# Attention backward over a KV cache: the last stores on GpSimd's queue, and a second-pass head beside each of the first pass's last two rows

## The chip, the cores and the metric
The kernel runs on one core of a Trainium2 chip. The metric is the device time of one execution in microseconds; 922.77 us is the median of three runs (921.22 to 922.89). Engines are named as the profile names them: PE (TensorE matmul), PEld (its weight load), DVE (VectorE), ACT (ScalarE), POOL (GpSimd) and SP (SyncE, which here only issues DMAs).

## What is computed
The reference is a decode step and its gradient. The forward part, cut to what matters:

```python
q = (layernorm(x) @ wq)                      # per head: 1 x 128
scores = einsum("bhqd,bhkd->bhqk", q, k) * Dh**-0.5
p = softmax(scores)
o = einsum("bhqk,bhkd->bhqd", p, v)
h = x + o @ wo
h2 = h + relu(layernorm(h) @ w1) @ w2        # the output
```

With B = 2, H = 32 heads of 128, and 4096 cached positions there are 64 pairs of batch and head, and each pair's K and V are 1 MB in bfloat16. `jax.vjp` asks for the gradients of all inputs. The two large ones have the shapes of the caches: gV is, for each pair, the outer product of p and the gradient of o; gK is the outer product of the scores' gradient and q. So 128 tiles of 1 MB are written, beside the gradients of wq, wo, w1 and w2 and that of x.

## The kernel before
The work on the caches has two passes, each going over the 64 pairs.

**First pass.** Row i loads K of pair i, and works on three pairs at once: the scores of pair i (PE transposes of K at L418, copies at L423, products at L429), the softmax and the scaled K of pair i-1 (`pk`, L480), and the sums over V of pair i-2 (`m_ps` L473, `u_ps` L502). So it has 66 rows, 0 to 65; the rows 64 and 65 only finish the last pairs. When V has been used, its tile goes back, or is kept for the second pass (the last 6 heads of batch 0 and the last 5 of batch 1).

**Second pass.** Head j (`p2_iter`, L848) reads V again as `W`, transposes it in pairs (L439), and multiplies it with the gradient of o (L452) for the scores' gradient `gsp` (L856). Then VectorE makes the two outer products in halves of about 1.2 us (`outer_half`, L834): in the call for head j, first gK of head j-1, then gV of head j. Each finished tile is stored by one DMA of 128 rows of 8 KB. `store_tile` (L839) chooses the queue: POOL while the list `queue` of loads still to be issued has entries, SP once it is empty. For the gK of heads 60, 61 and 62 it issues two DMAs, of rows 0 to 119 and of rows 120 to 127.

**What sets the order.** The order of all instructions is written by hand. `plan` (L1081 to L1089) pairs first-pass rows with second-pass heads: from row 41 on every second row has a head beside it (rows 41, 43, ..., 65 with heads 0 to 12), and when the first pass is over, from row 66 on, each row is one head. A closing row 64 of the second pass makes the last gK. From the same plan comes `queue` (L1092 to L1110), the order of the loads, which `pump` (L1111) issues on SP as soon as a load tile is free.

Loads and stores share a set of 1 MB tiles, which `share` hands out by use: `ld` for loads, `g` for gK and gV, `f` and `q` for the final gradients. The store tiles number three in the rows around 64, five from row 66 on (L1154), and seven from head 43 on (L1165). A tile is taken again in the order in which tiles were given back, and the instruction that writes it waits until its store has landed.

Beside the heads, background work is spread over the rows: the middle part of batch 1 (`middle_gen`), the outer products for the weights' gradients (`fin_gen`, L958, stored from ACT at L955), and the gradient of x (`gx_gen`, L983, with the products `ttr` of L660 on VectorE and two small stores at L655).

Of the kernel before, what the change touches and what calls it, by code (L numbers as in the profile page):

```python
# [15 lines left out]
def kernel(  # L16
# [20 lines left out]
    nc = tc.nc  # L37
# [35 lines left out]
    def pst(shape, dtype, role, name):  # L73

        k = banks[role].pop(0)
        banks[role].append(k)
        return ps.tile(shape, dtype, tag=f"bank{k}", bufs=1, name=name)
# [11 lines left out]
    def take(tag, shape, name):  # L89
        assert free[tag] > 0, (tag, name)  # L90
        free[tag] -= 1
        k = homes[tag].pop(0)
        t = pools[k].tile(shape, BF16, tag=f"big{k}", bufs=1, name=name)
        home_of[id(t)] = (tag, k, t)
        return t
# [9 lines left out]
    def give(t, to=None):  # L105
        tag, k, _ = home_of.pop(id(t))
        to = to or goes_to(tag)
        owned[tag] -= 1
        owned[to] += 1
        free[to] += 1  # L110
        homes[to].append(k)
        given_at[k] = step[0]
# [280 lines left out]
    NP1 = len(pairs)  # L393
# [37 lines left out]
    def pair_transpose(nat, g, dve=False, busy=0):  # L431


        t_ps = pst([128, GT // 2, 128], FP32, "tps", "t_ps")
        warm(t_ps[:].rearrange("p j k -> p (j k)"), nat, g, busy)
        natf = nat[:].bitcast(FP32)
        for j in range(GT // 2):
            cc = (g * GT) // 2 + j
            nc.tensor.transpose(t_ps[:, j, :], natf[:, 2 * cc:2 * cc + 2, :].rearrange("p c k -> p (c k)"), ident_f[:])  # L439
        t_sb = mats.tile([128, GT // 2, 128], FP32, tag="XT", bufs=5, name="t_sb")  # L440
        if dve:
            nc.vector.tensor_copy(out=t_sb[:], in_=t_ps[:])
        else:
            nc.scalar.copy(out=t_sb[:], in_=t_ps[:])  # L444
        return t_sb

    def pair_matvec(dst, t_sb, g, vecs):
        v = t_sb[:].bitcast(BF16).rearrange("p j (k two) -> p j k two", two=2)
        for j in range(GT // 2):
            sc = g * GT + 2 * j  # L450
            for par in range(2):
                nc.tensor.matmul(dst[:, sc:sc + 2], lhsT=v[:, j, :, par], rhs=vecs[:, par, :],  # L452
                                 start=(par == 0), stop=(par == 1))

    def natural(cache, b, h):
        return cache[b, h].rearrange("(p sc) d -> p sc d", sc=NSC)
# [375 lines left out]
    def outer_half(dst, row, colp, k):  # L832
        sl = slice(k * HALF, (k + 1) * HALF)
        nc.vector.tensor_tensor(  # L834
            out=pairs_view(dst[:, sl, :]),
            in0=row.rearrange("p (a two) -> p a two", two=2)[:, None, :, :].to_broadcast([128, HALF, 64, 2]),
            in1=colp[:, sl, None, :].to_broadcast([128, HALF, 64, 2]), op=ALU.mult)

    def store_tile(dst, t, uneven=False):  # L839

        eng = nc.gpsimd if queue else nc.sync
        if uneven:
            eng.dma_start(out=dst[0:120], in_=t[0:120])
            eng.dma_start(out=dst[120:128], in_=t[120:128])
        else:
            eng.dma_start(out=dst, in_=t[:])  # L846

    def p2_iter(j, busy):  # L848

        c = S2[j] if j < NP1 else None  # L850
        p = S2[j - 1] if j >= 1 else None
        if p is not None:
            bp, hp = turns[j - 1]
            pair_matvec(p["dp"], p.pop("T3"), 3, gom[:, hp, bp, :, :])
            gsp = small.tile([128, NSC, 2], BF16, tag="gsp", name="gsp")
            nc.vector.scalar_tensor_tensor(  # L856
                out=gsp[:], in0=p["dp"][:, :, None].to_broadcast([128, NSC, 2]), scalar=negdot[:, hp, bp:bp + 1],
                in1=P_bf[:, bp * H + hp, :, None].to_broadcast([128, NSC, 2]), op0=ALU.add, op1=ALU.mult)
        if c is not None:
            b, h = turns[j]  # L860
            go = gom[:, h, b, :, :]

            bank = pst([128, 512], FP32, "sps", "dp_ps")
            for k, col in enumerate((goc, qsc)):
                nc.tensor.matmul(bank[:, 128 + k * 128:256 + k * 128],  # L865
                                 lhsT=col[:, h, b:b + 1].to_broadcast([128, 128]), rhs=ident_bf[:],
                                 start=True, stop=True)
            c["dp"] = bank[:, 0:NSC]
            rb = mats.tile([128, 256], BF16, tag="rb", bufs=4, name="rb")
            nc.scalar.activation(out=rb[:], in_=bank[:, 128:384], func=ACT.Copy, scale=rt[:, b, h:h + 1])  # L870
            pp = small.tile([128, NSC, 2], BF16, tag="pp", name="pp")
            nc.gpsimd.tensor_copy(out=pp[:], in_=P_bf[:, b * H + h, :, None].to_broadcast([128, NSC, 2]))
            c.update(rb=rb, pp=pp)
            c["T0"] = pair_transpose(c["W"], 0, busy=busy)
        if p is not None:
            gK = take("g", [128, NSC, 128], "gK")
            outer_half(gK, p["rb"][:, 128:256], gsp, 0)
        yield
        if p is not None:
            outer_half(gK, p["rb"][:, 128:256], gsp, 1)  # L880
            store_tile(natural(out_2, bp, hp), gK, NP1 - 4 <= j - 1 < NP1 - 1)
            give(gK)
            del S2[j - 1]
        yield
        if c is None:
            return
        c["T1"] = pair_transpose(c["W"], 1, busy=busy)
        pair_matvec(c["dp"], c.pop("T0"), 0, go)
        yield
        c["T2"] = pair_transpose(c["W"], 2, busy=busy)  # L890
        pair_matvec(c["dp"], c.pop("T1"), 1, go)
        yield
        c["T3"] = pair_transpose(c["W"], 3, busy=busy)
        give(c["W"], "g" if j < H and j != 1 and owned["g"] < 3 else None)
        pair_matvec(c["dp"], c.pop("T2"), 2, go)
        gV = take("g", [128, NSC, 128], "gV")
        outer_half(gV, c["rb"][:, 0:128], c["pp"], 0)
        yield
        outer_half(gV, c["rb"][:, 0:128], c["pp"], 1)
        store_tile(natural(out_3, b, h), gV)  # L900
        give(gV)
        yield

# [173 lines left out]
    P2_AT = H + 2 + M0_ITERS  # L1077
# [4 lines left out]
    i = j = 0  # L1082
    while i <= NP1 + 1 or j <= NP1:
        ii = i if i <= NP1 + 1 else None
        jj = j if i > NP1 + 1 or (i >= P2_AT and (i - P2_AT) % 2 == 0) else None
        plan.append((ii, jj))
        i += 1
        if jj is not None:
            j += 1  # L1089


    queue = []  # L1092
# [51 lines left out]
    for n, (i, j) in enumerate(plan):  # L1144
# [21 lines left out]
        if j is not None:  # L1166
            while g2 is not None:
                p2_step()
            if j < NP1:
                bg_until(("go", *turns[j]))  # L1170
            g2 = p2_iter(j, 0)
# [93 lines left out]
```

## Time and profile before

| what | value |
|---|---|
| median of three runs | 922.77 us |
| the profiled execution | 922.89 us, span 921.1 us |
| busy share: PE, DVE, ACT, POOL | 82%, 75%, 58%, 18% |
| granted TensorE clock, mean | 0.771 |
| moved by DMA | 363.00 MB, mean 394 GB/s |
| read from HBM, written to it | 212.16 MB, 149.13 MB |
| gV and gK stores issued from POOL | 57 and 57, median 14.7 and 14.0 us to landing |
| gV stores issued from SP | 7, median 10.1 us to landing |
| VectorE waits for a stored tile | 18.3 us before gK, 17.9 us before gV |

The first column of a timeline row is the start in microseconds from the start of the span, the second the duration. In a table by stage each row is a stretch of the span; behind the busy times of the five engines come the granted TensorE clock, the mean busy share of the 16 DMA engines, and the rate in GB/s. A share may come out a little over 1, since successive packets overlap by a few nanoseconds. Queue q0 (software_dynamic) is POOL's, q1 (hardware_dynamic) SP's, and q10 ACT's. "Landing" is the time from a DMA's issue until its semaphore is complete, which takes all its engines.

### The profile page before, as it was taken

To read this page: it belongs to the slowest core of one execution; us is meant where nothing else is said; L and a number is where in the kernel's file an instruction comes from. 1 tells how busy PE (TensorE), PEld (TensorE's weight loads), DVE (VectorE), ACT (ScalarE), POOL (GpSimd) and SP (SyncE) were. 2 spreads that over 40 slices of the span, in tenths; PEclk is the share of its full clock that TensorE was granted. 3 is DMA by queue.
4 is the path that set the end of the run, shared out by engine and by line. 5 is a ranking of instruction groups with operands and counts; after the bars stand their busy time and mean duration, and the time that the engine had idled before them with its cause. 6 is when DMAs were issued, how large, how long until landed. Compare 5 with 4: busy or idle time off the path is not lost.

```text
span 921.1 us, 26511 instructions
## 1 busy us (share of the span) xinstructions
PE 756.2 (82%) x11226; PEld 633.7 (69%) x11226; DVE 692.7 (75%) x1291; ACT 531.8 (58%) x1096; POOL 162.8 (18%) x315
## 2 busy tenths in 40 slices
PE   5998998999989898988978837776788889588670
PEld 5887787888878787877868726665666666466360
DVE  4664786877779787767877989787796379999663
ACT  4665454667677776766733616445656666476450
POOL 1222222223201110010011112121221111111100
PEclk9999998999999999989985857565655555565555
DMA  9999999999779999999999999999999999999987
GB/s 347 417 398 409 407 395 409 412 418 341 296 300 345 412 414 424 422 422 422 412 396 402 418 426 410 397 396 405 414 384 397 389 397 423 425 425 424 425 322 265
DMA packets 59499, 363.00 MB, mean 394 GB/s; under 512 B 5717, under 2 KB 15573, under 8 KB 19189
## 3 DMA queue, kind: packets, MB, share of 16 engines
q1 hardware_dynamic: 39957, 226.86, 61.9%
q0 software_dynamic: 16416, 119.54, 31.4%
q10 hardware_dynamic: 3008, 14.91, 4.1%
q8 instruction: 88, 1.44, 0.6%
q14 instruction: 30, 0.25, 0.1%
HBM read 212.16 MB, written 149.13 MB: 392 GB/s over the span
## 4 chain that ended last, share of the span: by engine, by line
PE 39%; DMA 30%; DVE 17%; ACT 8%; issue 5%; POOL 0%; DVEq 0%; SPq 0%; ACTq 0%; POOLq 0%
DMA out_dram<-gK 11%; DMA Vt<-in_A_v_cache_dram 11%; PE m_ps L473 8%; PE t_ps L418 8%; PE t_ps L439 8%; DMA out_dram<-gV 6%; DVE gV L834 5%; ACT t_sb L423 4%; PE s_ps L429 3%; DVE gK L834 3%; PE u_ps L502 3%; DMA wqs<-in_A_wq_dram 2%; DVE junk L660 2%; DVE pk L480 2%; PE dp_ps L452 2%
## 5 line engine op out<-in xcount | busy, mean ns | idle before, releaser
L423 ACT COPY t_sb<-t_ps 128x1024 bf16<-128x1024 bf16 x223 | 217.7, 1017 | 46.4 <-PE t_ps L418 45.9
L444 ACT COPY t_sb<-t_ps 128x512 f32<-128x512 f32 x256 | 149.9, 587 | 148.8 <-PE t_ps L439 145.1
L439 PE MATMUL t_ps<-ident_f,Wt 128*128 128x128 f32 x848 | 201.8, 388 | 1.4 <-ACT t_sb L423 1.4
L480 DVE TENSOR_TENSOR pk<-Kt,ep 128x2048 bf16<-128x2048 bf16 x128 | 156.3, 1221 | 56.8 <-ACT ep L528 26.6
L473 PE MATMUL m_ps<-pk,Vt 128*128 128x129 bf16 x2048 | 172.1, 223 | 14.4 <-DMA Vt<-in_A_v_cache_dram 11.1
L834 DVE TENSOR_TENSOR gV<-rb,pp 128x2048 bf16<-128x2048 bf16 x128 | 152.8, 1218 | 22.4 <-DMA out_dram<-gK 17.9
L834 DVE TENSOR_TENSOR gK<-rb,gsp 128x2048 bf16<-128x2048 bf16 x128 | 152.2, 1224 | 20.2 <-DMA out_dram<-gV 18.3
L418 PE MATMUL t_ps<-ident_bf,Kt 128*128 128x128 bf16 x2048 | 156.9, 227 | 8.9 <-DMA Kt<-in_A_k_cache_dram 3.5
L439 PEld LDWEIGHTS t_ps<-ident_f,Wt 128*128 128x128 f32 x848 | 139.7, 201 | 28.7 <-issue 22.7
L473 PEld LDWEIGHTS <-Vt 128*128 128x128 bf16 x2048 | 125.5, 99 | 45.6 <-issue 30.5
L418 PEld LDWEIGHTS <-Kt 128*128 128x128 bf16 x2048 | 128.7, 102 | 16.3 <-issue 8.7
L452 PEld LDWEIGHTS <-t_sb 128*128 128x128 bf16 x2048 | 97.3, 107 | 39.7 <-ACT t_sb L444 18.4
L452 PE MATMUL dp_ps<-gom,t_sb 128*128 128x2 bf16 x2048 | 95.8, 168 | 9.5 <-ACT t_sb L444 8.8
L490 POOL COPY pk<-ep 128x16 bf16<-128x16 bf16 x80 | 63.1, 791 | 194.0 <-ACT ep L528 162.8
L429 PE MATMUL s_ps<-qc,t_sb 128*128 128x1 bf16 x2048 | 88.4, 164 | 1.4 <-DVE t_sb L421 1.2
L429 PEld LDWEIGHTS <-t_sb 128*128 128x128 bf16 x2048 | 78.2, 97 | 4.0 <-DVE t_sb L421 1.3
L953 ACT CAST ot<-o_ps 128x512 bf16<-128x512 f32 (+4 forms) x160 | 70.4, 488 | 17.7 <-DMA out_dram<-ot 9.4
L846 POOL DMA_DIRECT2D out_dram<-gV x57 | 30.5, 536 | 251.3 <-DVE gV L834 209.3
L846 POOL DMA_DIRECT2D out_dram<-gK x57 | 30.4, 533 | 248.0 <-DVE gK L834 198.3
L587 ACT CAST MT<-m_ps 128x128 bf16<-128x128 f32 x64 | 17.1, 267 | 76.1 <-PE m_ps L473 76.0
L870 ACT ACTIVATE rb<-dp_ps,rt 128x256 bf16<-128x256 f32 x64 | 30.4, 475 | 46.6 <-PE dp_ps L865 45.7
L660 DVE CUSTOM_DVE_ANT_0 junk<-wo_t,hbc 128x640 bf16<-128x640 bf16 x64 | 52.3, 818 | 0.2
(194 smaller groups left out, 779.2 us busy)
## 6 DMA issues: line engine op xcount, KB each, us to landing
Kt<-in_A_k_cache_dram SPq DMA_DIRECT2D x64, 1024.0 KB, 14.9
Vt<-in_A_v_cache_dram SPq DMA_DIRECT2D x64, 1024.0 KB, 13.6
out_dram<-gV POOLq DMA_DIRECT2D x57, 1024.0 KB, 14.7
out_dram<-gK POOLq DMA_DIRECT2D x57, 1024.0 KB, 14.0
Wt<-in_A_v_cache_dram SPq DMA_DIRECT2D x53, 1024.0 KB, 14.3
out_dram<-gV SPq DMA_DIRECT2D x7, 1024.0 KB, 10.1
wo_t<-in_A_wo_dram SPq DMA_DIRECT2D x4, 1280.0 KB, 19.4
wqs<-in_A_wq_dram SPq DMA_DIRECT2D x5, 1024.0 KB, 19.6
```

The source lines that it names most:

```text
L418: nc.tensor.transpose(t_ps[:, j, :], nat[:, g * GT + j, :], ident_bf[:])
L423: nc.scalar.copy(out=t_sb[:], in_=t_ps[:])
L429: nc.tensor.matmul(dst[:, sc:sc + 1], lhsT=t_sb[:, j, :], rhs=vec, start=True, stop=True)
L439: nc.tensor.transpose(t_ps[:, j, :], natf[:, 2 * cc:2 * cc + 2, :].rearrange("p c k -> p (c k)"), ident_f[:])
L444: nc.scalar.copy(out=t_sb[:], in_=t_ps[:])
L452: nc.tensor.matmul(dst[:, sc:sc + 2], lhsT=v[:, j, :, par], rhs=vecs[:, par, :], start=(par == 0), stop=(par == 1))
L473: nc.tensor.matmul(r["m"][:, 0:129], lhsT=r["V"][:, sc, :], rhs=r["pk"][sc // HALF][:, sc % HALF, 0:129], start=(sc == 0), stop=(sc == NSC ...
L480: nc.vector.tensor_tensor(out=p["pk"][k][:, :, 0:128].rearrange("p s (a two) -> p s a two", two=2), in0=p["K"][:, sl, :].rearrange("p s (a ...
L490: nc.gpsimd.tensor_copy(out=col, in_=e)
L660: nc.vector.tensor_tensor_reduce(out=junk[0:kc, 0:width], in0=in0, in1=in1, scale=1.0, scalar=0.0, op0=ALU.mult, op1=ALU.add, accum_out=acc)
L834: nc.vector.tensor_tensor(out=pairs_view(dst[:, sl, :]), in0=row.rearrange("p (a two) -> p a two", two=2)[:, None, :, :].to_broadcast([128 ...
L953: nc.scalar.copy(out=ot[0:P, k, n0:n0 + nn], in_=o_ps[0:P, 0:nn])
```

## The change
The plan gives row 64 a head too, so that rows 63, 64 and 65 carry the heads 11, 12 and 13, and all later heads come one row earlier. `store_tile` is gone: every gK and gV is stored from POOL, whole. The number of store tiles is as before.

```diff
-    def store_tile(dst, t, uneven=False):
-
-        eng = nc.gpsimd if queue else nc.sync
-        if uneven:
-            eng.dma_start(out=dst[0:120], in_=t[0:120])
-            eng.dma_start(out=dst[120:128], in_=t[120:128])
-        else:
-            eng.dma_start(out=dst, in_=t[:])
-
     def p2_iter(j, busy):
...
             outer_half(gK, p["rb"][:, 128:256], gsp, 1)
-            store_tile(natural(out_2, bp, hp), gK, NP1 - 4 <= j - 1 < NP1 - 1)
+            nc.gpsimd.dma_start(out=natural(out_2, bp, hp), in_=gK[:])
             give(gK)
...
         outer_half(gV, c["rb"][:, 0:128], c["pp"], 1)
-        store_tile(natural(out_3, b, h), gV)
+        nc.gpsimd.dma_start(out=natural(out_3, b, h), in_=gV[:])
         give(gV)
...
         ii = i if i <= NP1 + 1 else None
-        jj = j if i > NP1 + 1 or (i >= P2_AT and (i - P2_AT) % 2 == 0) else None
+        jj = j if i >= NP1 or (i >= P2_AT and (i - P2_AT) % 2 == 0) else None
         plan.append((ii, jj))
```

In the order of the built programs, 17 DMA instructions on SP (11 whole stores and 3 in two pieces) become 14 on POOL, each POOL store now stands between two `pp` copies (L872), and on SP the loads W of heads 12 and 13 stand ahead of V of pairs 62 and 63.

## The prediction
> **What bounds the kernel now.** I read the page's 40 slices first, then a table by stage, the DMA queues of two short stretches, and last the timeline of SP's queue at the end. On the page the DMA row shows 9 (90% or more busy) nearly everywhere after 400 us, and moves 395 to 425 GB/s; no compute engine comes near that. From row 64 on, the time is what 16 DMA engines need for the bytes, plus every stretch in which they are idle or slow. So the question for each part of the change is: does it change the bytes, or the idle and slow stretches?
>
> The bytes don't change. The table by stage (times, busy time of PE, PEld, DVE, ACT, POOL, granted clock, DMA share, GB/s) shows where the slow stretches are:
>
> ```profile
> 455.00:465.00 10.00, 8.88 (x175) 7.58 (x173) 8.44 (x19) 5.67 (x16) 1.47 (x3) 1.00 0.95 372
> 495.00:505.00 10.00, 7.65 (x113) 7.36 (x112) 5.39 (x8) 2.35 (x4) 2.57 (x5) 0.50 1.01 421
> ...
> 850.00:860.00 10.00, 4.39 (x29) 2.55 (x27) 8.52 (x12) 3.75 (x8) 3.19 (x4) 0.50 1.02 426
> ...
> 888.00:890.00 2.00, 0.37 (x3) 0.37 (x3) 1.97 (x4) 0.00 (x0) 0.24 (x1) 0.50 0.07 29
> 890.00:892.00 2.00, 2.00 (x18) 1.78 (x17) 2.00 (x3) 1.26 (x3) 0.00 (x0) 0.50 0.95 393
> 892.00:894.00 2.00, 2.00 (x22) 1.88 (x22) 2.00 (x3) 0.97 (x2) 0.00 (x0) 0.50 0.89 271
> 894.00:896.00 2.00, 1.46 (x24) 1.38 (x21) 1.97 (x4) 1.06 (x2) 0.00 (x0) 0.50 0.98 254
> 896.00:898.00 2.00, 2.00 (x17) 1.72 (x17) 2.00 (x2) 1.17 (x2) 0.00 (x0) 0.50 0.95 254
> ...
> 912.00:914.00 2.00, 0.00 (x0) 0.00 (x0) 0.00 (x0) 0.00 (x0) 0.00 (x0) 0.50 1.03 401
> ```
>
> Up to about 886 us the DMA is full at 425 GB/s. At 888 to 890 its share is 0.07, one engine in 16: a single engine that is late works alone while the others are empty. At 892 to 898 the engines are busy (0.89 to 0.98) but move only 254 to 271 GB/s: each packet takes longer. When no uneven store is left (912 to 914), the rate is 401 again. The timeline of SP's queue says what was issued then:
>
> ```profile
> 889.41 0.33 SPq L846 DMA_DIRECT2D out_dram<-gV  x1
> ...
> 892.12 0.35 SPq L843 DMA_DIRECT2D out_dram<-gK  x1
> 892.52 0.50 SPq L844 DMA_DIRECT2D out_dram<-gK  x1
> 894.39 0.58 SPq L846 DMA_DIRECT2D out_dram<-gV  x1
> ...
> 899.25 3.15 SPq L846 DMA_DIRECT2D out_dram<-gV  x1
> 902.49 1.91 SPq L843 DMA_DIRECT2D out_dram<-gK  x1
> ```
>
> The slow stretch begins with the first uneven store (L843, L844). The trace's packet records agree: 8 KB packets last 310 ns on average at 840 to 885 us (2 of 1830 over 450 ns), 399 ns at 890 to 910 (173 of 741), 328 ns after 910.5. Just before the uneven store, packets of the whole store of 889.41 still last 307 to 341 ns. Why the others stretch isn't shown; that they do while uneven stores are under way is.
>
> **Part 1: the last 14 stores, POOL instead of SP, whole instead of split.** The end is set by the late engine. Of the last POOL store (issued 853.37) 15 engines landed by 877.2 us, one at 886.9; the last packet of the run ends at 919.74 on one engine, 2.2 us after the others. Followed through the packet records, the late engine is never empty, and starts the tile stored at 889.41 at 892.8 us. From there it needs 26.9 us for the last eight tiles: 8 packets each, 64 x 0.309 = 19.8 us (8192 B at 425/16 = 26.6 GB/s is 0.308 us), one instruction fetch of 0.94 us at 898.2, and 6.2 us more. These 6.2 us are 3 x 0.31 for a packet of each of the three 8-row pieces, and 5.3 us of stretch. With whole stores both go: **-6.2 us**, its last packet at 913.5.
>
> What could give it back? (a) Issue: a POOL store takes 533 ns and starts about 0.3 us after its VectorE half, an SP one takes 332 ns and starts at once: 0.5 us later per store, and where POOL's queue stood empty its first packet came 1.3 to 4.1 us after the issue began (seven cases). Behind a backlog this costs nothing: seven store tiles turn around in 7 x 2.47 = 17.3 us of the engines' time, while issue, first packet, landing and 2.4 us on VectorE take some 9. Without cover the last store would pay up to 4 us. (b) On POOL, pp of the next head (L872, 0.24 to 0.41 us) now stands behind the gV store: it is ready 0.3 + 0.53 + 0.41 = 1.2 us after gV, and VectorE first has gsp and gK, 0.28 + 2.36 us. Hidden. If not, 1.2 us a row. (c) Can POOL's queue carry the whole rate? Here it did, alone (packets, MB, share):
>
> ```profile
> DMA packets 528, 3.84 MB, mean 427 GB/s; under 512 B 59, under 2 KB 59, under 8 KB 59
> ...
> q0 software_dynamic: 526, 3.84, 101.2%
> ```
>
> That is 544 to 553 us. At 890 to 906 SP's queue, alone, moved 313 GB/s at 94.3% share. So the queue itself costs 0.
>
> A rule speaks against this part. The Trainium skill's page SBUF — State Buffer (SBUF: two separate sides) says that VectorE in a two-port mode keeps GpSimd from writing a DMA's descriptors, so that the transfer waits, and advises the SP or ACT queue; VectorE is 98% busy here. The case's row is 0.3 us from VectorE's end to POOL's issue and 427 GB/s with VectorE at 90%; by the rule up to 2.4 us a store would be lost, by the row nothing, and the row decides.
>
> A second page also speaks for the split: DMA: Bandwidth & Descriptors (Why a DMA increments its semaphore by 16 and not by 1; Latency and other measured facts) lets 120 rows use 15 engines and 8 rows 8, and calls engines 7 and 15 usually slower, so the split would spare a slow one. That is the last rival below.
>
> **Part 2: a head beside row 64 (and 65).** Every head from 12 on comes one row earlier, and there are 117 rows instead of 118. No instruction is added but what follows from the order: on SP the loads W12 and W13 go ahead of V62 and V63 (order of the two programs), so each V comes one 1 MB load later, 2.5 us at 424 GB/s. PE waits for V already (L473, 11.1 us in six waits). While the DMA is full such a wait moves nothing: bounds 0 and +2.5 us. The gain: the DMA share is 0.95 at 455 to 465 and 1.01 after it, so at most 0.6 us of idle can be filled. Rows 64 and 65 still have three store tiles (five from row 66, seven from head 43): gK12 needs gV11's tile, back at 474.7 in the trace, as it does now. VectorE then waits in row 65, where the first pass has no pk left for it. I take **0** (nearest: the share of 1.01), bounds -0.6 and +2.5. The background work (final outer products, gx) falls one head later; its last stores go out at heads 61 and 62, well ahead of the end. Where the buffers change hands at 665 to 740 us the share falls to 0.78 to 0.95 in places, 3 us of idle in all; half as much either way, 1.5 us, may shift.
>
> **Sum.** Profiled execution 922.89 (span 921.13 and 1.76 around it): 922.89 - 6.2 + 0 = 916.7. The median of the runs is 0.12 lower, so I predict **916.6 us**.
>
> **Rivals.**
> *The whole rate comes back.* If the late engine catches up as others idle less, the end is the mean engine's. From 890 us 8.47 MB were moved (sum of the table); at 425 that is 19.9 us, and the 2.8 us hole at 886 to 890 goes too: the last packet at 907.1, 12.6 us earlier, **910.2**. For: DMA share 1.01 is a mean over all engines. Against: the late engine has its own backlog, and it alone was working at 888. 0.10.
>
> *Compute takes over the end.* The last heads cost VectorE 4.95 us each (899.45 to 904.31, gK to gK), PE about the same, while two tiles need 4.94 us of DMA. Heads with final outer products took PE 8.8 us (862.2 to 871.0), and now reach one head further. If waits put VectorE's last gK at its old 906.7 plus one 3.8 us, the store adds 0.8 issue, 4.1 to the first packet, 2.5, 1.4 to the span's end: 919.3, time **921.1**. For: VectorE is 98% busy at 800 to 860. Against: it idled 17 us for returned tiles at 855 to 907. 0.17.
>
> *The changed order costs in the middle.* V loads later and three store tiles for two heads in a row: one wait like the 10.6 us for gV's tile at 464 (chain of waits), not covered, less 6.2: **927.3**. It decides if the DMA share falls under 0.9 for 10 us at 460 to 490. Against: loads are queued nine tiles deep. 0.07.
>
> *The late engine is the one the split spares (slower).* Then its 26.9 us held only 40 packets, and 24 more come back at 0.309: +7.4, **930.3**. It decides if that engine has no part in the 120-row pieces. Against: the piece issued at 902.49 landed last at 914.8 and its 8-row piece at 915.2, as late against the others (912.6, 912.7) as the next whole store (917.7 against 915.1). 0.11.
>
> **Numbers.** My forecast has 0.55 (916.6, give or take 2.5 for first packets and part 2). What a measurement can tell from no change is 0.2%, 1.8 us, so faster means under 920.9. Faster: 0.55 + 0.10 + 0.04 of the compute case = 0.69; same: 0.12 (the rest of that case up to 924.6); slower: 0.07 + 0.11 and 0.01 = 0.19. The range 910 to 924 takes in the first three cases and leaves out the last two, 0.18.
>
> **What would show it.** After: no stretch under 380 GB/s from 885 us to the end; 8 KB packets at 0.31 us there; no share of 0.07; the last gK made about 900 and its store landing a dozen us later. Wrong, if the last store's issue to landing is under 8 us (then compute sets the end), if the share falls at 460 to 490, or if one engine still lands over 6 us after the others at the end.

## The result, and the profile after

The changed kernel took 914.13 us (median of four runs, 913.67 to 914.43); the kernel before, run beside it, 922.00 (919.22 to 922.89). The ratio is 0.9919, with a 95% interval of 0.9896 to 0.9942; the forecast was 916.6 us. The profiled execution took 914.32 us, 912.4 of it the span.

| | before | after |
|---|---|---|
| last half of the last gK ends on VectorE | 906.7 us | 896.0 us |
| last packet of the last store ends | 919.74 us | 910.26 us |
| VectorE waits for a stored tile, from 845 us on | 16.4 us | 3.0 us |
| moved by DMA, mean rate | 363.00 MB, 394 GB/s | 363.00 MB, 398 GB/s |

The same bytes are moved, so the question is again which stretches were idle or slow. VectorE's waits from 845 us on are these two lines (total, times, longest):

```profile
DVE gK L834 <- DMA out_dram<-gV: 2.8, 1, 2.8
DVE gV L834 <- DMA out_dram<-gK: 0.2, 1, 0.2
```

The table by stage of the changed kernel has the same columns as the one of the kernel before:

```profile
455.00:465.00 10.00, 9.30 (x178) 8.27 (x171) 8.51 (x15) 4.58 (x14) 2.02 (x3) 1.00 0.96 370
465.00:475.00 10.00, 6.67 (x113) 5.62 (x111) 5.65 (x6) 4.90 (x12) 1.31 (x3) 1.00 1.01 420
475.00:485.00 10.00, 2.89 (x37) 2.74 (x37) 6.53 (x14) 0.57 (x1) 1.31 (x3) 0.61 0.98 414
485.00:495.00 10.00, 9.34 (x94) 8.65 (x93) 9.41 (x23) 4.74 (x10) 1.91 (x5) 0.50 0.99 371
850.00:860.00 10.00, 8.64 (x68) 5.07 (x66) 7.05 (x10) 7.08 (x14) 1.46 (x3) 0.63 1.01 418
...
888.00:890.00 2.00, 1.70 (x28) 1.47 (x27) 1.68 (x3) 1.55 (x3) 1.70 (x2) 1.00 1.01 414
890.00:892.00 2.00, 1.62 (x31) 1.29 (x30) 1.90 (x2) 1.17 (x2) 0.53 (x1) 1.00 1.04 422
892.00:894.00 2.00, 0.17 (x7) 0.07 (x4) 1.97 (x4) 0.00 (x0) 0.25 (x1) 0.89 0.98 401
894.00:896.00 2.00, 0.00 (x0) 0.00 (x0) 2.00 (x2) 0.00 (x0) 0.29 (x1) 0.50 1.02 426
896.00:898.00 2.00, 0.00 (x0) 0.00 (x0) 0.05 (x1) 0.00 (x0) 0.53 (x1) 0.50 0.98 410
898.00:900.00 2.00, 0.00 (x0) 0.00 (x0) 0.00 (x0) 0.00 (x0) 0.00 (x0) 0.50 1.02 426
900.00:902.00 2.00, 0.00 (x0) 0.00 (x0) 0.00 (x0) 0.00 (x0) 0.00 (x0) 0.50 0.88 369
902.00:904.00 2.00, 0.00 (x0) 0.00 (x0) 0.00 (x0) 0.00 (x0) 0.00 (x0) 0.50 0.37 156
904.00:906.00 2.00, 0.00 (x0) 0.00 (x0) 0.00 (x0) 0.00 (x0) 0.00 (x0) 0.50 0.17 74
906.00:908.00 2.00, 0.00 (x0) 0.00 (x0) 0.00 (x0) 0.00 (x0) 0.00 (x0) 0.50 0.06 25
908.00:910.00 2.00, 0.00 (x0) 0.00 (x0) 0.00 (x0) 0.00 (x0) 0.00 (x0) 0.50 0.07 29
```

Read the two last columns downward. The stretch with 0.07 at 888 is gone, and so are the rows in which the engines were busy and moved only 254 GB/s: share and rate now belong together (0.98 with 410, 1.02 with 426). From 900 on the share falls, though no engine has anything left to make: the last tile was stored at 896. The other engines run out one by one, and from 906 on the share is 0.06 to 0.07, one engine of 16, until the end. The late engine is still late. (The trace does not number the engines; the late one is the one on which a tile lands last.) The packet records show that the slow packets are gone: at 890 to 905 us those of 8 KB took 315 ns on average, 3 of 644 over 450 ns; before it was 401 ns, 134 of 559.

The timeline of POOL's queue shows what was issued at the end:

```profile
885.95 0.53 POOL L872 DMA_DIRECT2D out_dram<-gK  x1 [2.71 <-DVE gK L834]
888.22 0.53 POOL L891 DMA_DIRECT2D out_dram<-gV  x1 [1.74 <-DVE gV L834]
888.75 1.17 POOL L863 COPY pp<-P_bf 128x64 bf16<-128x64 bf16 x1
891.30 0.53 POOL L872 DMA_DIRECT2D out_dram<-gK  x1 [1.38 <-DVE gK L834]
893.75 0.53 POOL L891 DMA_DIRECT2D out_dram<-gV  x1 [1.92 <-DVE gsp L847]
896.34 0.53 POOL L872 DMA_DIRECT2D out_dram<-gK  x1 [2.06 <-DVE gK L834]
```

Each store is one whole DMA of 533 ns. The last one has its landing on 15 engines by 906.4 us and on the last engine at 910.7, 14.3 us after the issue. So compute was over 14 us ahead of the end, and what was left was a queue of stores.

### The profile page after: what moved, and what is told of

Its sections match the earlier page's. It is cut to its first block, busy times and chain, and to the rows that moved or that the text cites. A ratio compares the mean times of both kernels' runs of the same rounds, so it can differ in the third digit from the quotient of the medians.

```text
span 912.4 us, 26504 instructions
## 1 busy us (share of the span) xinstructions
PE 739.9 (81%) x11226; PEld 619.8 (68%) x11226; DVE 693.5 (76%) x1291; ACT 530.5 (58%) x1096; POOL 174.2 (19%) x329
## 2 busy tenths in 40 slices
DMA packets 59479, 363.00 MB, mean 398 GB/s; under 512 B 5697, under 2 KB 15553, under 8 KB 19169
## 4 chain that ended last, share of the span: by engine, by line
PE 38%; DMA 26%; DVE 18%; ACT 10%; issue 6%; POOL 1%; SPq 0%; POOLq 0%; ACTq 0%; DVEq 0%
DMA Vt<-in_A_v_cache_dram 12%; PE t_ps L439 8%; PE m_ps L473 8%; PE t_ps L418 7%; DMA out_dram<-gV 6%; DVE gV L834 5%; DMA out_dram<-gK 5%; ACT t_sb L423 4%; DVE gK L834 3%; PE s_ps L429 3%; ACT t_sb L444 3%; DMA wqs<-in_A_wq_dram 3%; DVE pk L480 3%; DVE junk L660 2%; PE u_ps L502 2%
## 5 line engine op out<-in xcount | busy, mean ns | idle before, releaser
L439 PE MATMUL t_ps<-ident_f,Wt 128*128 128x128 f32 x848 | 190.7, 370 | 2.1 <-ACT t_sb L423 2.1
L834 DVE TENSOR_TENSOR gK<-rb,gsp 128x2048 bf16<-128x2048 bf16 x128 | 152.5, 1225 | 29.1 <-DMA out_dram<-gV 27.1
L834 DVE TENSOR_TENSOR gV<-rb,pp 128x2048 bf16<-128x2048 bf16 x128 | 152.9, 1218 | 18.4 <-DMA out_dram<-gK 16.3
L418 PE MATMUL t_ps<-ident_bf,Kt 128*128 128x128 bf16 x2048 | 153.1, 224 | 8.6 <-DMA Kt<-in_A_k_cache_dram 3.4
L439 PEld LDWEIGHTS t_ps<-ident_f,Wt 128*128 128x128 f32 x848 | 131.6, 192 | 35.9 <-issue 28.1
L418 PEld LDWEIGHTS <-Kt 128*128 128x128 bf16 x2048 | 125.6, 100 | 16.2 <-issue 9.1
L452 PEld LDWEIGHTS <-t_sb 128*128 128x128 bf16 x2048 | 95.5, 106 | 44.2 <-issue 18.9
L490 POOL COPY pk<-ep 128x16 bf16<-128x16 bf16 x80 | 66.4, 833 | 189.0 <-ACT ep L528 154.5
L891 POOL DMA_DIRECT2D out_dram<-gV x64 | 34.3, 535 | 272.0 <-DVE gV L834 195.0
L872 POOL DMA_DIRECT2D out_dram<-gK x64 | 34.1, 533 | 260.5 <-DVE gK L834 202.0
L429 PEld LDWEIGHTS <-t_sb 128*128 128x128 bf16 x2048 | 77.6, 97 | 4.2 <-ACT t_sb L423 1.2
## 6 DMA issues: line engine op xcount, KB each, us to landing
wqs<-in_A_wq_dram SPq DMA_DIRECT2D x5, 1024.0 KB, 19.8
```

Of the source, the lines that this page charges most:

```text
L418: nc.tensor.transpose(t_ps[:, j, :], nat[:, g * GT + j, :], ident_bf[:])
L429: nc.tensor.matmul(dst[:, sc:sc + 1], lhsT=t_sb[:, j, :], rhs=vec, start=True, stop=True)
L490: nc.gpsimd.tensor_copy(out=col, in_=e)
L834: nc.vector.tensor_tensor(out=pairs_view(dst[:, sl, :]), in0=row.rearrange("p (a two) -> p a two", two=2)[:, None, :, :].to_broadcast([128 ...
```

## The experiments

Three things came together in the change: the queue, the split by rows, and the row shift. The theory on record was that the split costs the time and the queue and the shift nothing. The rivals are that the queue brings the gain, since stores on POOL let VectorE go on sooner (last gK 10.7 us earlier), or that the shift does. All runs below stand against runs of the kernel before on the same chip, whose times there went from 915.1 to 925.7 us. The ratio is taken from the single runs, so it is not the quotient of the two medians beside it.

| kernel | queue at the end | gK of heads 60 to 62 | shift | median us, before beside it | ratio, 95% interval |
|---|---|---|---|---|---|
| e1_row | SP | 120 + 8 rows | yes | 919.03, 919.94 | 1.0005 [0.9976, 1.0035] |
| e2_pool_whole | POOL | whole | no | 915.51, 919.94 | 0.9961 [0.9940, 0.9983] |
| e3_sp_whole | SP | whole | no | 914.05, 919.94 | 0.9941 [0.9918, 0.9963] |
| e4_pool_split | POOL | 120 + 8 rows | no | 921.13, 919.94 | 1.0012 [0.9994, 1.0030] |
| e5_changed | POOL | whole | yes | 915.54, 921.35 | 0.9932 [0.9911, 0.9952] |
| e6_row_sp_whole | SP | whole | yes | 912.84, 921.35 | 0.9915 [0.9886, 0.9945] |
| e7_even_pieces | SP | 64 + 64 rows | no | 920.84, 921.35 | 1.0006 [0.9981, 1.0031] |
| e8_six_split | SP | 120 + 8 rows, heads 57 to 62 | no | 928.59, 921.35 | 1.0083 [1.0055, 1.0111] |
| e9_columns | SP | two halves of the columns | no | 913.62, 920.71 | 0.9922 [0.9903, 0.9940] |
| e10_pool_whole_2 | POOL | whole | no | 914.23, 920.71 | 0.9930 [0.9907, 0.9953] |
| e11_changed_2 | POOL | whole | yes | 915.98, 920.71 | 0.9947 [0.9929, 0.9966] |

**One part alone: shift, stores, queue, split.** Four kernels.

e1_row has only the shift:

```diff
-        jj = j if i > NP1 + 1 or (i >= P2_AT and (i - P2_AT) % 2 == 0) else None
+        jj = j if i >= NP1 or (i >= P2_AT and (i - P2_AT) % 2 == 0) else None
```

> Only the plan changes: row 64 has a head, the stores stay as before (SP for the last 14, three gK in two pieces). The prediction's theory: the DMA is full around the rows 64 to 66, so this alone is worth 0 (-0.6 to +2.5 us, ratio 0.999 to 1.003). Rival: the changed kernel moved 3.5 us more between 720 and 750 us, so the row shift gives 3 to 5 us by another meeting of heads and background work (ratio 0.995 to 0.997), and in its trace the lead over before appears in that stretch.

e2_pool_whole has only the stores of the change (POOL, whole):

```diff
-        eng = nc.gpsimd if queue else nc.sync
+        eng = nc.gpsimd
...
-            store_tile(natural(out_2, bp, hp), gK, NP1 - 4 <= j - 1 < NP1 - 1)
+            store_tile(natural(out_2, bp, hp), gK)
```

> Only the stores change: all from POOL, whole; the plan is as before. The prediction's theory: -6.2 us (ratio 0.993), all of it after 885 us, with 8 KB packets at 0.31 us there. Rival (the row shift has half of the gain): -4 to -5 us here (0.995), the rest in e1_row. If both edits only work together: ratio 1.000 here.

e3_sp_whole leaves the queue as it was and drops only the split:

```diff
-            store_tile(natural(out_2, bp, hp), gK, NP1 - 4 <= j - 1 < NP1 - 1)
+            store_tile(natural(out_2, bp, hp), gK)
```

> The last 14 stores stay on SP, but the gK of heads 60 to 62 are stored whole. The prediction's theory (the two pieces stretch the packets, the queue itself costs nothing): about the same as e2_pool_whole, -6 us (0.993), packets at 0.31 us after 890 us. Rival (SP's queue is what is slow at the end, and passes the stores that wait on POOL's): no gain, ratio 0.999 to 1.001, and the stretch under 320 GB/s after 890 us stays.

e4_pool_split changes only the queue and keeps the split:

```diff
-        eng = nc.gpsimd if queue else nc.sync
+        eng = nc.gpsimd
```

> All stores from POOL, but the gK of heads 60 to 62 in two pieces of 120 and 8 rows; the plan is as before. The prediction's theory: the stretch comes back, packets at about 0.4 us, so 5 to 6 us slower than e2_pool_whole and near before (ratio 0.998 to 1.002). Rival (the pieces matter only on SP's queue): as e2_pool_whole, 0.993.

The shift alone gave nothing (1.0005), the queue alone nothing (1.0012). Without the split there was a gain on either queue (0.9961 and 0.9941). The slow packets go with the split: at 890 to 905 us, 106 of 572 over 450 ns in e1 and 144 of 561 in e4, 1 of 755 in e2 and 3 of 749 in e3. The table by stage of e4, stores on POOL in pieces:

```profile
892.00:894.00 2.00, 0.00 (x0) 0.00 (x0) 1.97 (x3) 0.00 (x0) 0.20 (x1) 0.50 1.00 279
...
900.00:902.00 2.00, 0.00 (x0) 0.00 (x0) 0.00 (x0) 0.00 (x0) 0.00 (x0) 0.50 0.99 274
```

and that of e3, whole stores on SP:

```profile
886.00:888.00 2.00, 0.58 (x4) 0.58 (x4) 1.97 (x4) 0.17 (x1) 0.24 (x1) 0.50 0.11 45
888.00:890.00 2.00, 2.00 (x18) 1.78 (x17) 2.00 (x4) 1.30 (x3) 0.00 (x0) 0.50 1.04 432
...
894.00:896.00 2.00, 2.00 (x21) 1.66 (x20) 2.00 (x3) 1.17 (x2) 0.00 (x0) 0.50 0.98 397
896.00:898.00 2.00, 1.46 (x23) 1.31 (x21) 1.97 (x3) 1.17 (x2) 0.00 (x0) 0.50 0.99 401
```

A share of 1.00 with 279 GB/s stands on POOL's queue, a share of 0.98 with 397 on SP's: the slowness belongs to the pieces. It does not come from long issues either: in the kernel before SP's issues took 1.5 to 3.2 us each from 899 us on (0.33 us in e3), but in e4 POOL issued the same pieces in 0.50 to 0.53 us each, and e4 is as slow. And e3 still has the hole: 0.11 at 886 to 888. Its VectorE waits for stored tiles as it did in the kernel before:

```profile
DVE gV L834 <- DMA out_dram<-gK: 10.0, 4, 3.9
DVE gK L834 <- DMA out_dram<-gV: 6.4, 3, 3.9
```

This is the wait list of e3 from 845 to 907 us (total, times, longest): 16.4 us, where the changed kernel has 3.0. Yet e3's last packet ends at 911.4 us and e2's, with no hole and 3.7 us of such waits, at 910.8. e4 shows the reverse: its VectorE waits for no stored tile in that stretch and makes the last gK by 894.4 us, 12.3 us before the kernel before does, and the time stays (1.0012). A hole in which the late engine works on, and an engine that waits meanwhile, cost nothing here; the late engine's own packets do. In e3 the margin was some 3 us: its last store, issued at 904.5, had landed on 14 engines by 908.8 and on the last two at 910.4 and 911.8.

**The shift once the stores are whole.** e5_changed is the changed kernel again, e6_row_sp_whole is e3 with the shift; later e10_pool_whole_2 (e2 again) ran beside e11_changed_2 (the changed kernel).

> The changed kernel again, in one call with the combinations. If the row shift is worth nothing, it stands where e2_pool_whole stood (ratio 0.996, interval 0.994 to 0.998); if the 3.5 us it moved earlier between 720 and 750 us reach the end once the uneven pieces are gone, 0.991 to 0.993.

> Row 64 has a head, and the last 14 stores go whole from SP. If the row shift adds to whole stores: as e5_changed, or 1 us better, since an SP store starts 0.5 us sooner (0.990 to 0.992). If the row shift is worth nothing: as e3_sp_whole (0.994).

> The same kernel as e2_pool_whole (whole stores on POOL, the plan as before), beside the changed kernel on one chip, to settle the row shift. If the shift is worth nothing, this and the changed kernel give the same ratio within 0.002, about 0.994. If the shift gives some 3 us once the stores are whole, this stays at 0.996 and the changed kernel is 0.003 lower.

> The changed kernel once more, beside e10. Shift worth nothing: the same ratio as e10 within 0.002, about 0.994. Shift worth some 3 us: 0.993 or less, 0.003 under e10, and its DMA moves ahead of e10's between 720 and 750 us, where the tiles change hands.

e5 and e6 came out 0.003 under e2 and e3, and their traces had more bytes moved at 720 to 740 us, where the tiles change hands, so the shift looked worth some 3 us. The direct pair e10 and e11 turned this round: 0.9930 without the shift, 0.9947 with it, intervals overlapping. Over the four comparisons each, whole stores without the shift (e2, e3, e9, e10) average 0.9939, with it (the result, e5, e6, e11) 0.9928: 0.001, or 1 us, less than a measurement of this kernel can tell. The stage itself, in the kernel before and then in the changed one:

```profile
720.00:730.00 10.00, 6.90 (x54) 4.86 (x52) 4.03 (x5) 6.22 (x13) 0.53 (x1) 0.50 0.93 393
730.00:740.00 10.00, 9.32 (x96) 6.37 (x94) 3.54 (x5) 6.66 (x14) 0.78 (x2) 0.50 0.95 357
```

```profile
720.00:730.00 10.00, 8.90 (x71) 6.42 (x70) 5.00 (x6) 6.57 (x13) 1.31 (x3) 0.50 1.01 424
730.00:740.00 10.00, 6.61 (x60) 5.07 (x59) 4.31 (x6) 5.26 (x11) 1.31 (x3) 0.50 1.01 426
```

and e9, which has the plan of before:

```profile
720.00:730.00 10.00, 8.84 (x85) 7.10 (x85) 4.92 (x5) 6.67 (x14) 1.31 (x3) 0.55 1.01 426
730.00:740.00 10.00, 8.59 (x88) 5.72 (x86) 5.09 (x6) 6.25 (x16) 1.30 (x3) 0.62 1.02 426
```

At 426 GB/s in both rows, e9 has the full rate there without the shift. The five profiles with the shift moved 8.48 to 8.52 MB in these 20 us, the eight without it 7.50 to 8.52. So a profile of before at 7.50 (this one) and one of after at 8.50 differ by 1.0 MB, or 2.4 us at 425 GB/s, and this difference can't be put down to the change alone. Whether the shift makes the good case more frequent, its mean worth up to 1 us, stays open.

**Uneven pieces, or any pieces?** After the first four runs the theory went further: the 120 + 8 split is bad because it is uneven. e7_even_pieces splits the same three gK in halves, and e8_six_split doubles the number of uneven stores.

```diff
-            eng.dma_start(out=dst[0:120], in_=t[0:120])
-            eng.dma_start(out=dst[120:128], in_=t[120:128])
+            eng.dma_start(out=dst[0:64], in_=t[0:64])
+            eng.dma_start(out=dst[64:128], in_=t[64:128])
```

> As before, but the gK of heads 60 to 62 in two pieces of 64 rows each. Theory A (it is the uneven spread of rows over the engines that stretches packets): no stretch, as e3_sp_whole, 0.994. Theory B (it is two DMAs for one tile, whatever their rows): packets at about 0.4 us after 890 us and no gain, 0.999 to 1.002.

```diff
-            store_tile(natural(out_2, bp, hp), gK, NP1 - 4 <= j - 1 < NP1 - 1)
+            store_tile(natural(out_2, bp, hp), gK, NP1 - 7 <= j - 1 < NP1 - 1)
```

> As before, but six gK (heads 57 to 62) in pieces of 120 and 8 rows instead of three. If the price belongs to each uneven store (5.3 us of stretch for three, and their one more packet), three more cost about 5 us: ratio 1.005 to 1.007. If it arises only when the engines have no other work to do, nothing more: 0.999 to 1.002.

e8 went the way the price foretold, and a little further than the 1.005 to 1.007 expected: 0.0083 of 921.35 is 7.6 us for three more uneven stores, 2.5 each (1.7 to 3.4 by the interval). e7 went against the theory: even halves cost as much as 120 + 8. Its table by stage:

```profile
892.00:894.00 2.00, 0.00 (x0) 0.00 (x0) 2.00 (x3) 0.00 (x0) 0.00 (x0) 0.50 0.98 279
894.00:896.00 2.00, 0.00 (x0) 0.00 (x0) 1.97 (x3) 0.00 (x0) 0.00 (x0) 0.50 0.92 234
```

234 to 279 GB/s at a share over 0.9, as with the uneven pieces. Of its 8 KB packets that started at 892 to 898 us, half took 309 to 315 ns, a quarter 585 ns and more. So unevenness isn't it. Two causes were left: a split by rows, or two DMAs for one tile.

**Rows, or two DMAs?** e9_columns keeps two DMAs for each of the three tiles and splits them by columns, 128 rows of 4 KB each:

```diff
-            eng.dma_start(out=dst[0:120], in_=t[0:120])
-            eng.dma_start(out=dst[120:128], in_=t[120:128])
+            eng.dma_start(out=dst[:, 0:16, :], in_=t[:, 0:16, :])
+            eng.dma_start(out=dst[:, 16:32, :], in_=t[:, 16:32, :])
```

> The kernel before with one thing changed: the gK of heads 60, 61 and 62 are still two DMAs each on SP, but split by columns (all 128 rows x 4 KB, twice) instead of by rows (120 and 8). If it is the split by rows that costs (rows then lie with other DMA engines than in a whole store, and packets stretch), this is as fast as whole stores on SP: 0.994, some 5 us less than before, with few packets over 450 ns for 8 KB after 890 us. If it is two DMAs for one tile that cost (issue, descriptors, a second landing), no gain: 0.999 to 1.001. 96 more packets of 4 KB per tile instead of 8 KB ones may cost something by themselves, by no row of this case so far; a time between the two would say so.

It was as fast as whole stores, 0.9922 [0.9903, 0.9940]. Its table by stage:

```profile
892.00:894.00 2.00, 1.81 (x24) 1.44 (x22) 2.00 (x3) 1.23 (x3) 0.00 (x0) 0.77 0.93 379
894.00:896.00 2.00, 0.35 (x8) 0.27 (x8) 1.97 (x4) 0.15 (x1) 0.00 (x0) 1.00 1.02 410
896.00:898.00 2.00, 0.00 (x0) 0.00 (x0) 2.00 (x3) 0.00 (x0) 0.00 (x0) 0.58 1.08 436
```

379 to 436 GB/s, with 1 of 426 packets of 8 KB over 450 ns and 4 KB packets at 163 ns, half of a whole one. Two DMAs for a tile cost nothing; giving each of them a part of the rows cost time in both forms tried.

The Trainium skill's page DMA: Bandwidth & Descriptors (The descriptor swizzle) says that in a transfer into 128 rows of the on-chip memory each DMA engine has the rows behind one port for itself, and SBUF — State Buffer (Door 1: The DMA port swizzle) that rows 0 to 63 lie behind only 8 of the 16 ports. If a store, which reads such rows, is spread over the engines in the same way, then 64 rows over 16 engines put two engines on one port, and a split by columns leaves each engine its port. The runs agree with that in all five forms tried (whole, columns, 64 + 64, 120 + 8 on either queue), and the stretched packets of about twice 309 ns fit; but no run shows a port, nor on which side of the transfer, the on-chip memory or HBM, the packets are held up. So the mechanism behind the stretch is argued, not shown.

## Why the prediction was right, and where not

**Part 1, the mechanism: right.** The split cost the time and the queue cost none (e3 against e4). **Its size:** -6.2 us was forecast. The medians of the result differ by 7.9 us; the three comparisons of the changed kernel (the result, e5, e11) average 0.9933, which is 6.2 us. The average of the four kernels with whole tiles or columns and the old plan, 0.9939 of some 920.7 us, is 5.6 us. In the two traces the late engine's last 64 packets of 8 KB, which were put at 26.9 us with the pieces and 19.8 without, took 19.7 us (890.6 to 910.3). That is 7.2 us less, of which 0.9 is an instruction fetch that the sum kept and that didn't fall there. The engine ended at 910.3 and not at 913.5, because it also came to these packets 2.2 us sooner (890.6 for 892.8); that is about what the two profiles differ by at 720 to 740 us, though no run ties the two together. Neither the missing fetch nor the earlier start was in the forecast; they are what this pair of profiles shows beyond 6.2 us. That the average of 6.2 meets the forecast to the tenth is luck, since each ratio is known to about 2 us. One step of the sum is not shown: from 898 to 907 us in the kernel before a tile's last two landings are 0.1 to 1.2 us apart, so that one and the same engine was last all the way can't be read from the trace.

**Its two terms.** The 0.9 us for packets of the 8-row pieces was not separated by a run; the 64 + 64 pieces, each with 16 landings in the trace, so four rows an engine, should give no engine more packets than a whole store does, and the kernel with them is as slow as with 120 + 8 (1.0006). So the stretch of 5.3 us alone can fill the whole price.

**What hides POOL's later issue:** right. The last store was issued at 896.3 and landed at 910.7, behind a backlog of stores. POOL's queue moved 401 to 426 GB/s at 888 to 896 us with VectorE busy for 1.7 to 2.0 of each 2 us; e2 and e3, alike but for the queue, differ by 0.002 with overlapping intervals. On POOL the copy `pp` of the changed kernel took 1.17 us at 888.75 and not 0.24 to 0.41; it stayed hidden, since it ended at 889.9 and VectorE came to gV at 891.1, straight after gK. The rule of the Trainium skill's page SBUF — State Buffer (SBUF: two separate sides), that VectorE keeps GpSimd from writing descriptors, is stated for VectorE's two-port modes. The prediction counted it against this part without showing that the outer products (TENSOR_TENSOR, L834) run in such a mode, and no run here shows it; so these runs don't test the rule, and show only that POOL's stores beside this work cost no time.

**Part 2, taken at 0:** right by e1 (1.0005). The share at 455 to 485 us is 0.96 to 1.01, as foretold.

**What would show it.** Packets at 0.31 us and no hole at 888: as foretold. The last gK was made at 896.0 and not about 900, since the waits for returned tiles fell to 3.0 us; e3 and e4 show that this is the queue's doing (last gK 904.4 and 894.4 us). Two signs were put wrongly. "No stretch under 380 GB/s from 885 us to the end" and "no share of 0.07" don't hold after 900 us: the forecast itself had a late engine, which must leave such a tail. It was 4.3 us, under the 6 that would have spoken against it.

**The rivals.** The whole rate did not come back: 15 engines were done at 906.4, near the 907.1 of that rival, and the late one set the end. Compute did not take over (last gK 14 us ahead of the end). The order cost nothing in the middle. The late engine is not the one that the split spares: with whole stores its last eight tiles took 7.2 us less, not 7.4 more. In the trace of the kernel before the 8-row pieces land on 8 engines and the 120-row pieces on 15, as the prediction took it; but the late engine had part in both. Two readings beside the rivals are off, and nothing rests on them: at 800 to 860 us VectorE is busy for 57.9 of 60 us, which is 96% and not 98%, and gK to gK from 899.45 to 904.31 is 4.86 us and not 4.95.

**Left open:** why one engine is late. It is in before and after, whether the last stores go from SP or from POOL, and with whole stores as with pieces; up to about 850 us all these kernels store gV and gK from POOL, so which queue makes it late is not shown. In all these traces there are packets of 16 KB for instruction fetch (88 in after, 0.6% of 16 engines by the table of queues). They don't all go to the late engine: one of 0.93 us started at 891.61 in after, while that engine's landings at 890.98 and 893.56 are 2.6 us apart, and eight packets take 2.5. No run tried to relieve the late engine.

## What to carry to other kernels

Where DMA is the bound, read share and rate together: a share near 1 at 254 to 280 GB/s beside 425 elsewhere means that packets stretch, and the shape of the transfers is to be looked at, not the queue. A store of 128 rows that has to be cut should be cut by columns: here that was free, while three tiles cut by rows cost some 5.6 us. When one engine ends last, holes in which only it works are no loss as long as the others still end before it, and filling them (here by another queue, which brought VectorE 10 us forward) gains nothing.

## What the runs showed of the hardware that was not expected

- Both splits by rows that were tried stretched packets, the even one too: 64 + 64 rows gave a mean of 431 ns for 8 KB at 890 to 905 us (158 of 518 over 450 ns), 120 + 8 rows 401 ns, whole stores 312 to 317 ns, halves of the columns 319 ns. Packets of whole stores beside the pieces are in these means.
- One kernel's profiles differ where nothing differs in the program: with the plan of before, 7.50 to 8.52 MB were moved at 720 to 740 us, up to 2.4 us of DMA time; e2 and e10, the same program, moved 7.59 and 8.20. A single pair of profiles can't be read closer than that.
